# Rooms by rank: sorting the experts of a routed layer on the chip and giving each a room of its own size

## The chip, the core and the metric

The kernel runs on one core of a Trainium2 chip. The metric is the time of one execution in device microseconds (us); the time before is 1312.08 us, the median of three runs (1309.42 to 1315.21).

The engines of the core, by the names that the profile uses: PE is TensorE's matmul, PEld its weight load, DVE is VectorE, ACT is ScalarE, POOL is GpSimd, SP is SyncE, which issues most of the DMAs. Each engine executes its own stream in order; a letter q behind a name (SPq) is the engine's sequencer.

## The reference

Three stages, one after another, all in float32.

1. Attention of 4 batches, 8 heads, 576 positions, head size 64. In each row of scores only the 32 largest are kept before the softmax.
2. A gated layer: with x of 2304 tokens by 512, `(x @ w_a) * (x @ w_b) @ w_out`, inner width 1536.
3. A routed layer with 8 experts. Each token goes to the expert whose embedding is nearest in direction; its output is scaled by the softmax weight of that expert:

```
expert_idx = np.argmax(logits, axis=1)
gate_w = probs[np.arange(N), expert_idx]
for e in range(E):
    mask = expert_idx == e
    h = np.maximum(x[mask] @ w1[e], 0.0)          # w1[e]: 512 x 1024
    out[mask] = gate_w[mask, None] * (h @ w2[e])  # w2[e]: 1024 x 512
```

How many tokens an expert gets is known only when the routing has run.

## The kernel before, in words

Attention and gated layer are interleaved: the attention's scores, top-32 search and softmax set a step order that the program writes out by hand for PE, DVE, ACT and POOL, and matmuls of the gated layer (groups of 256 tokens, `moe1`) fill PE's gaps. All products are made of three float32r products of high and low parts (`TERMS`).

When a chunk of 128 tokens leaves the gated layer, `route` (L760) runs in small steps between other work, 18 chunks in all. It stores the row in `xr`, computes norms, logits, the softmax sum, the expert, and the token's rank in its expert from a running count `base8` (128 equal rows of 8 counts). The row with its softmax sum in column `DM` goes to DRAM (`row_d`, L801), and its token number is scattered by an indirect DMA (L819) into the list of its expert, `ids_d`, which has 2560 places per expert.

Then the experts run, in a second part in which only PE's order is by hand; the order of the other engines and of SP's queue comes from a scheduler that plays the program through in an estimated time and lets instructions move ahead of others where their inputs are there, by priority.

- `first_expert` (L1154) computes the first 256 tokens of expert 0, which are known before the last chunks are routed.
- `last_tile` (L1222) computes the rest of expert 0's room, rows 256 to 335. It also gathers the rows of the next expert (`gather`, L1216, three indirect DMAs by `pick`) and turns them (`turn_x`, L1103: four PE transposes, an ACT copy of the high part, a DVE subtraction for the low part).
- The loop at L1269 does experts 1 to 7 with a room of `cap` = 336 columns each. Stage 1 (`stage1`, L1126) has 8 blocks of 12 matmuls, weights stationary, `cap` columns moving; stage 2 (L1284) has 4 blocks of 24 with `cap` columns and, in the last expert alone, tiles of tokens stationary (`stage2`). Results of the others are turned back (`back`) in the next expert's stage 1.
- `put` (L1114) takes the reciprocal of the softmax sum (DVE, L1115), scales the result on ACT and scatters the rows to the output by an indirect DMA on POOL. Rows past an expert's count are dummies: they read a zero row and are dropped in the scatter.
- Weights come in units of 1 MB, four per expert, through two raw buffers (`unit`, L1047; DMA on SP at L1061, for the first four in quarters at L1058), and ACT and DVE split them into high and low parts in four buffers `u`. `upto` starts units four ahead.
- The ids of all experts are loaded by seven DMAs on SP (L1212) when the last scatter of `ids_d` has landed.
- At the end a loop guarded by a register (L1353, `more`) computes tiles of any expert that has more than 336 tokens (`extra`). With the reference's inputs it does not run.

## Time and profile before

| | us |
|---|---|
| median of the runs | 1312.08 |
| profiled execution | 1318.34 |
| its span | 1316.50 |
| PE busy / PEld busy | 1170.2 / 1008.8 |
| DVE, ACT, POOL busy | 933.3, 819.9, 726.1 |
| DMA moved | 240.58 MB, mean 183 GB/s |

The span is that of the profiler's records, from the first to the last. Three stretches can be told apart: to about 870 us the attention, with DVE busy nearly all of the time; to about 1050 us the rest of the gated layer and the first tiles of expert 0; from 1081 to 1306 us experts 1 to 7. Busy time of PE counts overlapping matmuls by a modelled end, so the pace of matmuls is read from the distance of their starts. The granted clock is in parts of 2.4 GHz: 1.00 is 2.4 GHz, 0.50 is 1.2 GHz.

### The profile page before, as it was taken

How to read it: one execution, taken by the hardware profiler on the slowest of the kernel's cores; microseconds unless marked ns; L12 is line 12 of the kernel's file. 1: busy time of each engine (PE TensorE's matmuls, PEld its weight loads, DVE VectorE, ACT ScalarE, POOL GpSimd, SP SyncE). 2: the span in 40 equal slices, each digit the busy share in tenths (PEclk: the TensorE clock that was granted, in tenths of full speed). 3: DMA queues.
4: the chain of work that ended last, by engine and by line, in shares of the span. 5: the costliest groups of instructions: out<-in, count | busy, mean ns of one | idle time of the engine just before them, and what ended most of it. 6: DMA issues, size and time to landing. Idle time of an engine off the chain costs nothing. (4 is left out here: it accounts for less than half of the span.)

```text
span 1316.5 us, 23808 instructions
## 1 busy us (share of the span) xinstructions
PE 1170.2 (89%) x8124; PEld 1008.8 (77%) x8125; DVE 933.3 (71%) x2019; ACT 819.9 (62%) x1964; POOL 726.1 (55%) x1188
## 2 busy tenths in 40 slices
PE   5667978879999987999998998899999989999996
PEld 3445655667888766888887886777988869999995
DVE  8998998989889889999988898740200136555550
ACT  5876888777767776777777776663532335444441
POOL 5655886667667775676777766564544320222211
PEclk8887999989999997999999999899999989999998
DMA  7433775557686645667665767458987045555530
GB/s 227 141 108 123 249 234 179 193 166 216 201 248 184 178 151 180 194 195 204 199 191 160 213 185 213 128 158 277 333 285 232 32 125 169 176 175 175 177 113 23
DMA packets 129102, 240.58 MB, mean 183 GB/s; under 512 B 24621, under 2 KB 73901, under 8 KB 128978
## 3 DMA queue, kind: packets, MB, share of 16 engines
q1 hardware_dynamic: 124818, 228.74, 56.1%
q0 software_dynamic: 4160, 10.29, 2.2%
q8 instruction: 65, 1.06, 0.3%
q14 instruction: 59, 0.48, 0.1%
HBM read 198.92 MB, written 40.85 MB: 182 GB/s over the span
## 5 line engine op out<-in xcount | busy, mean ns | idle before, releaser
L387 DVE MAX8 t<-y 128x8 f32<-128x576 f32 x432 | 312.2, 750 | 3.0
L402 POOL TENSOR_TENSOR z<-s,z 128x576 f32<-128x576 f32 x144 | 206.2, 1432 | 105.0 <-ACT z L399 100.2
L390 DVE MATCH_REPLACE8 y<-t,y 128x576 f32<-128x576 f32 x288 | 213.9, 743 | 0.0
L722 PE MATMUL ab<-xg,wab 128*128 128x256 f32 x1398 | 205.6, 289 | 7.4 <-ACT gab L736 3.1
L722 PEld LDWEIGHTS ab<-xg,wab 128*128 128x128 f32 x1398 | 181.8, 190 | 11.3 <-ACT gab L736 3.5
L722 PE MATMUL ab<-raw,wab 128*128 128x256 f32 x1152 | 173.4, 291 | 8.1 <-ACT gab L736 5.0
L421 PE MATMUL tr<-ident,z 128*128 128x128 f32 x720 | 133.6, 285 | 37.2 <-ACT z L404 31.2
L722 PEld LDWEIGHTS ab<-raw,wab 128*128 128x128 f32 x1152 | 151.7, 192 | 12.3 <-ACT gab L736 5.9
L404 ACT ACTIVATE z<-z,bi 128x576 f32<-128x576 f32 x144 | 111.7, 775 | 69.9 <-POOL z L402 69.9
L366 PE MATMUL tr<-kT,qT 128*128 128x288 f32 x512 | 128.0, 333 | 25.8 <-ACT qT L343 13.7
L387 DVE MAX8 t<-s 128x8 f32<-128x576 f32 x144 | 107.6, 747 | 51.5 <-ACT s L367 43.2
L367 ACT ACTIVATE s<-tr 128x288 f32<-128x288 f32 x288 | 119.0, 414 | 33.4 <-PE tr L366 32.1
L424 ACT ACTIVATE wt<-tr 128x384 f32<-128x384 f32 (+2 forms) x320 | 128.0, 415 | 16.3 <-PE tr L421 15.6
L1117 POOL DMA_INDIRECT out_dram<-o,ids x24 | 31.4, 1307 | 190.4 <-DVE u L1068 107.1
L669 PE MATMUL x<-wo,gh 128*128 128x512 f32 x432 | 135.8, 395 | 0.0
L656 POOL TENSOR_TENSOR gab<-gab 128x256 f32<-128x256 f32 x108 | 82.6, 765 | 92.1 <-ACT gab L736 80.5
L421 PEld LDWEIGHTS tr<-ident,z 128*128 128x128 f32 x720 | 90.1, 145 | 54.2 <-ACT z L404 35.8
L1068 DVE TENSOR_TENSOR u<-raw,u 128x1024 fp32r<-128x1024 f32 x64 | 75.9, 1222 | 77.6 <-ACT u L1067 55.2
L366 PEld LDWEIGHTS tr<-kT,qT 128*128 128x128 f32 x512 | 87.4, 204 | 38.8 <-ACT qT L343 16.1
L399 ACT ACTIVATE z<-s,bi 128x576 f32<-128x576 f32 x144 | 112.9, 784 | 0.6 <-DVE bi L392 0.6
L1133 PE MATMUL h<-xT,u 128*128 128x336 f32 x672 | 109.3, 319 | 0.0
L656 POOL TENSOR_TENSOR gl<-gab,gh 128x256 fp32r<-128x256 f32 x108 | 80.6, 747 | 49.8 <-ACT gh L656 37.7
(193 smaller groups left out, 2299.8 us busy)
## 6 DMA issues: line engine op xcount, KB each, us to landing
wab<-wab_d SPq DMA_DIRECT2D x192, 512.0 KB, 4.3
raw<-in_moe_w_dram SPq DMA_DIRECT2D x28, 1024.0 KB, 6.5
wab_d<-wab SPq DMA_DIRECT2D x24, 512.0 KB, 4.3
kT<-kT_d SPq DMA_DIRECT2D x20, 576.0 KB, 7.7
vs<-in_v_dram SPq DMA_DIRECT2D x36, 256.0 KB, 3.5
kT_d<-kT SPq DMA_DIRECT2D x16, 576.0 KB, 4.0
raw<-in_moe_w_a_dram SPq DMA_DIRECT2D x12, 512.0 KB, 4.2
raw<-in_moe_w_b_dram SPq DMA_DIRECT2D x12, 512.0 KB, 5.3
```

The lines of the kernel that those rows point to most:

```text
L366: pe.matmul(p, l, r, start=(i == 0), stop=(i == len(terms) - 1))
L367: act.activation(t.s[:, cs], p, AF.Copy, scale=SCALE)
L387: dve.max(v, cur)
L390: dve.match_replace(out=rest, in_to_replace=v, in_values=cur, imm_value=LOWEST)
L399: act.activation(t.w, t.s, AF.Relu, bias=t.bi[:, 1:2], scale=-HUGE)
L402: pool.tensor_tensor(t.w, t.s, t.w, op=OP.subtract)
L404: act.activation(t.w, t.w, AF.Exp, bias=t.bi[:, 0:1], accum_out=t.o.sm[:, t.slot : t.slot + 1])
L421: pe.transpose(pt[:, i * P : (i + 1) * P], t.w[:, k0 : k0 + P], ident)
L424: act.activation(th[:, sl, w], pv[:, :, src], AF.Copy)
L656: pend.pop(0)[1]()
L669: pe.matmul(px[t], g[:, ts], wo[:, w, f], start=(f == 0 and i == 0), stop=(f == NF - 1 and i == 2))
L722: pe.matmul(ps_[i], wt[:, a, c, :], xg[x][:, c, :], start=(j == 0 and f not in begun), stop=(j == len(terms) - 1),)
```

## The change

- Experts 1 to 7 are put in the order of their counts. With the last `base8` DVE forms a key, 8 x count + number, for each expert; expert 0 gets a key above all. One instruction sorts the eight keys in falling order; the lowest three bits are the expert's number.
- SP loads the seven numbers into registers (`values_load`, at the highest priority). The ids of the sorted experts are loaded with a register in the address, one DMA for each expert, and so are their weights (`unit`).
- Each place in the order has a room: `CAPS` = 336 for expert 0, then 336, 328, 312, 296, 280, 272, 264. Place 7, the smallest, runs first, place 1 last.
- The reciprocal of the softmax sum moves from `put` into `route`: the row in DRAM now holds the factor itself. The DVE instruction stands one step later in the routing than the sum, and the row's DMA behind it.
- The overflow test at the end compares each place's count with its room, and the guarded loop runs over places.

```diff
@@ -23,6 +23,8 @@
 LOWEST = -3.0e38
 STRIDE = 2560
 CAP = 336
+CAPS = (CAP, 336, 328, 312, 296, 280, 272, 264)
+FIRST = 2.0**20
 GROUPS = [(256 * i, 256) for i in range(9)]
 GN = 256
 SEQ = "0A 0B 1A 0T 1BT 2A 2BT 3AT 3B"
...
@@ -142,6 +144,9 @@
     pool.iota(e8i, pattern=[[1, NE]], base=0, channel_multiplier=0)
     e8 = cst.tile([P, NE], F32, name="e8")
     dve.tensor_copy(e8, e8i)
+    e8k = e8i.bitcast(F32)
+    dve.tensor_copy(e8k, e8)
+    dve.memset(e8k[:, 0:1], FIRST)
     e8s = cst.tile([P, NE], F32, name="e8s")
     dve.tensor_scalar(e8s, e8, float(STRIDE), None, op0=OP.mult)
 
...
@@ -797,14 +802,15 @@
             pool.tensor_copy(ohb, oh)
             yield 0.0
             pool.memset(xr[:, DM + 1 : RW], 0.0)
-            pool.tensor_tensor(xr[:, DM : DM + 1], st[:, 3:4], eps, op=OP.add)
-            sp.dma_start(row_d[1 + ch * P : 1 + (ch + 1) * P, :], xr)
+            pool.tensor_tensor(st[:, 6:7], st[:, 3:4], eps, op=OP.add)
             pr = mp.tile([P, 512], F32, name="ab", bufs=2)
             pe.matmul(pr[:, 0:NE], tri, ohb, start=True, stop=True)
             pe.matmul(pr[:, NE : 2 * NE], ones, ohb, start=True, stop=True)
             rk = mk.tile([P, 2 * NE], F32, name="rk")
             act.activation(rk, pr[:, 0 : 2 * NE], AF.Copy)
             yield 0.0
+            dve.reciprocal(xr[:, DM : DM + 1], st[:, 6:7])
+            sp.dma_start(row_d[1 + ch * P : 1 + (ch + 1) * P, :], xr)
             pool.tensor_tensor(rk[:, :NE], rk[:, :NE], base8, op=OP.add)
             pool.tensor_tensor(base8, rk[:, NE:], base8, op=OP.add)
             if ch == NCL - 1:
...
@@ -1046,12 +1052,13 @@
 
         def unit(i, pace=False):
 
-            e, part = divmod(i, 4)
+            n, part = divmod(i, 4)
+            e = slice(0, 1) if n == 0 else bass.ds(expert[NE - n], 1)
             raw = w2p.tile([P, 4, 512], F32, name="raw", bufs=2)
             if part < 2:
-                src = w1[e, :, part * 512 : (part + 1) * 512].rearrange("(c p) f -> p c f", p=P)
+                src = w1[e, :, part * 512 : (part + 1) * 512].rearrange("o (c p) f -> p (o c) f", p=P)
             else:
-                src = w2[e, (part - 2) * 512 : (part - 1) * 512, :].rearrange("(f p) d -> p f d", p=P)
+                src = w2[e, (part - 2) * 512 : (part - 1) * 512, :].rearrange("o (f p) d -> p (o f) d", p=P)
             if pace:
                 for c in range(4):
                     act.activation(raw[:, c, 0:1], recent[0][:, 0, 0:1], AF.Copy)
...
@@ -1081,8 +1089,12 @@
         wx = ph.enter_context(tc.tile_pool(name="wx", bufs=1, side="right"))
         banks = [ph.enter_context(tc.tile_pool(name="ps2", bufs=1, space=PSUM, side="right"))]
         TERMS = ((1, 0), (0, 1), (0, 0))
+        cap = max(caps)
         NT3 = -(-cap // P)
-        M = [min(P, cap - t * P) for t in range(NT3)]
+
+        def rows_of(r):
+
+            return [min(P, caps[r] - t * P) for t in range(NT3)]
         idv = ids_d.rearrange("(e r) c -> e r c", e=NE)
         turns = {"h": 0, "y": 0, "tr": 0}
 
...
@@ -1112,8 +1124,7 @@
             dve.tensor_tensor(lo, pv, hi.bitcast(F32), op=OP.subtract)
 
         def put(p, xg, ids, m, o):
-            dve.reciprocal(xg[:m, DM + 1 : DM + 2], xg[:m, DM : DM + 1])
-            act.activation(o[:m], p[:m], AF.Copy, scale=xg[:m, DM + 1 : DM + 2])
+            act.activation(o[:m], p[:m], AF.Copy, scale=xg[:m, DM : DM + 1])
             pool.indirect_dma_start(
...
@@ -1207,28 +1218,41 @@
             return
 
         wk = ph.enter_context(tc.tile_pool(name="wk2", bufs=2))
-        for es, ts in ((slice(0, 1), (NT3 - 1,)), (slice(1, 2), range(NT3)), (slice(2, NE), range(NT3))):
-            for t in ts:
-                sp.dma_start(ids[: M[t], es, t, :], idv[es, t * P : t * P + M[t], :].rearrange("e p c -> p e c"))
+        m0 = rows_of(0)[-1]
+        sp.dma_start(ids[0][:m0, NT3 - 1], idv[0, (NT3 - 1) * P : (NT3 - 1) * P + m0, :])
+        key = wx.tile([P, 2, 8], F32, name="key")
+        counts = wx.tile([P, 8], I32, name="counts")
+        place = wx.tile([P, 8], I32, name="place")
+        with tc.high_priority(offset=FG):
+            dve.scalar_tensor_tensor(key[:, 0], base8, 8.0, e8k, op0=OP.mult, op1=OP.add)
+            dve.max(key[:, 1], key[:, 0])
+            dve.tensor_copy(counts, key[:, 1])
+            dve.tensor_scalar(place, counts, 7, None, op0=OP.bitwise_and)
+            for r in range(NE - 1, 0, -1):
+                expert[r] = nc.values_load(place[0:1, r : r + 1], engines=[sp.engine], min_val=0, max_val=NE - 1)
+        for r in range(NE - 1, 0, -1):
+            sp.dma_start(
+                ids[r], idv[bass.ds(expert[r], 1), : NT3 * P, :].rearrange("o (t p) c -> p (o t) c", p=P)
+            )
 
         banks.append(ph.enter_context(tc.tile_pool(name="ps3", bufs=1, space=PSUM)))
 
-        def gather(e):
+        def gather(r):
             xs = [wx.tile([P, RW], F32, name="xg", bufs=2 * NT3) for _ in range(NT3)]
             for t in range(NT3):
-                pick(xs[t], t, ids[: M[t], e, t, 0:1])
-            return xs, [wk.tile([P, KC, cap], F32R, name=f"xT{i}") for i in range(2)]
+                pick(xs[t], ids[r][: rows_of(r)[t], t, 0:1])
+            return xs, [wk.tile([P, KC, cap], F32R, name=f"xT{i}")[:, :, : caps[r]] for i in range(2)]
 
         def last_tile():
 
-            t, m = NT3 - 1, M[-1]
+            t, m = NT3 - 1, m0
             xs = [None] * t + [wx.tile([P, RW], F32, name="xg", bufs=2 * NT3)]
-            xT = [wk.tile([P, KC, cap], F32R, name=f"xT{i}") for i in range(2)]
+            xT = [wk.tile([P, KC, cap], F32R, name=f"xT{i}")[:, :, : caps[0]] for i in range(2)]
             hT = [wk.tile([P, NF2, cap], F32R, name=f"hT{i}", bufs=1)[:, :, :m] for i in range(2)]
-            pick(xs[t], t, ids[:m, 0, t, 0:1])
-            nx = gather(1)
+            pick(xs[t], ids[0][:m, t, 0:1])
+            nx = gather(NE - 1)
             turn_x((xs, xT), t)
...
@@ -1254,35 +1278,37 @@
             for f in range(NF2):
                 stage2(0, f, p, hT[0][:, f], hT[1][:, f])
                 if f in FX:
-                    turn_x(nx, 1 + FX.index(f))
-            put(p, xs[t], ids[:m, 0, t, 1:2], m, result())
+                    turn_x(nx, 1 + FX.index(f), NE - 1)
+            put(p, xs[t], ids[0][:m, t, 1:2], m, result())
             return nx
 
-        def back(e, xs, yT, t):
-            m = M[t]
+        def back(r, xs, yT, t):
+            m = rows_of(r)[t]
...
+            hT = [wk.tile([P, NF2, cap], F32R, name=f"hT{i}", bufs=1)[:, :, :n] for i in range(2)]
             for f in range(NF2):
                 if f % 4 == 0:
                     upto(4 * e + f // 4 + UB)
-                for _ in stage1(e, f, xT, hT[0][:, f], hT[1][:, f], cap):
+                for _ in stage1(e, f, xT, hT[0][:, f], hT[1][:, f], n):
                     pass
                 if backs and f % 2 == 0:
                     backs.pop(0)()
                 if f == GF and e + 1 < NE:
-                    nx = gather(e + 1)
+                    nx = gather(r - 1)
             if e + 1 < NE:
-                yT = wx.tile([P, KC, cap], F32, name="yT", bufs=1)
+                yT = wx.tile([P, KC, cap], F32, name="yT", bufs=1)[:, :, :n]
                 for d in range(KC):
-                    p = bank("y")[:, :cap]
+                    p = bank("y")[:, :n]
                     for f in range(NF2):
                         if f % 4 == 0 and d == 0:
                             upto(4 * e + 2 + f // 4 + UB)
...
@@ -1338,24 +1364,27 @@
                 pe.matmul(p, hT[:, f, :], w2f[:, f, :], start=(f == 0), stop=(f == NF2 - 1))
             put(p, xg, ids[:, 1:2], P, result())
 
-        top = wk.tile([P, 8], F32, name="top", bufs=1)
-        dve.max(top, base8)
-        NX = -(-(NT - cap) // P)
-        need = wk.tile([P, NE, NX], I32, name="need", bufs=1)
-        lim = wk.tile([P, NX], I32, name="lim", bufs=1)
-        pool.iota(lim, pattern=[[P, NX]], base=cap, channel_multiplier=0)
-        limf = wk.tile([P, NX], F32, name="limf", bufs=1)
-        dve.tensor_copy(limf, lim)
-        for e in range(NE):
-            dve.tensor_scalar(need[:, e, :], limf, base8[:, e : e + 1], None, op0=OP.is_lt)
-        more = wk.tile([P, 1], I32, name="more", bufs=1)
-        dve.tensor_scalar(more, top[:, 0:1], float(cap), None, op0=OP.is_gt)
-        with tc.If(nc.values_load(more[0:1, 0:1], min_val=0, max_val=1) > 0):
-            with tc.For_i(0, NE, 1) as e:
-                with tc.For_i(0, NX, 1) as t:
-                    go = nc.values_load(need[0:1, bass.ds(e, 1), bass.ds(t, 1)], min_val=0, max_val=1)
-                    with tc.If(go > 0):
-                        extra(e, t)
+        starts = wx.tile([P, 8], I32, name="starts")
+        over = wx.tile([P, 8], I32, name="over")
+        for r, c in enumerate(caps):
+            pool.iota(starts[:, r : r + 1], pattern=[[0, 1]], base=c, channel_multiplier=0)
+        dve.tensor_scalar(over, counts, 3, None, op0=OP.logical_shift_right)
+        dve.tensor_scalar(over[:, 0:1], over[:, 0:1], int(FIRST) // 8, None, op0=OP.subtract)
+        dve.tensor_tensor(over, over, starts, op=OP.subtract)
+        dve.tensor_scalar(over, over, 0, None, op0=OP.max)
+        dve.tensor_copy(key[:, 0], over)
+        dve.max(key[:, 1], key[:, 0])
+        dve.tensor_copy(counts, key[:, 1])
+        with tc.If(nc.values_load(counts[0:1, 0:1], min_val=0, max_val=NT) > 0):
+            with tc.For_i(0, NE, 1) as r:
+                with tc.For_i(0, -(-(NT - min(caps)) // P), 1) as t:
+                    left = nc.values_load(over[0:1, bass.ds(r, 1)], min_val=0, max_val=NT)
+                    with tc.If(left > t * P):
+                        e = nc.values_load(place[0:1, bass.ds(r, 1)], engines=[sp.engine], min_val=0, max_val=NE - 1)
+                        first = nc.values_load(
+                            starts[0:1, bass.ds(r, 1)], engines=[sp.engine], min_val=min(caps), max_val=max(caps)
+                        )
+                        extra(e, first, t)
 
 
 _INS = ["q", "k", "v", "moe_w_a", "moe_w_b", "moe_w_out", "moe2_expert_emb", "moe2_tau", "moe2_w1", "moe2_w2"]
```

## Rows read from the trace of the kernel before

**Rows 1.** Busy by windows: us, PE PEld DVE ACT POOL (instructions), clock, DMA.
```profile
1100.00:1150.00 50.00, 50.00 (x338) 49.84 (x337) 27.05 (x40) 21.47 (x32) 9.17 (x8) 1.00 0.46 154
1250.00:1300.00 50.00, 50.00 (x311) 47.80 (x310) 19.34 (x31) 17.35 (x28) 8.17 (x7) 1.00 0.25 88
```
**Rows 2.** Timeline of PE: start, us, engine, line, operation, out<-in, sizes, count.
```profile
1041.63 6.65 PE L1133 MATMUL h<-xg,u 128*128 128x256 f32 x54
1048.11 5.75 PE L1145 MATMUL y<-u,wab 128*128 128x512 f32 x24
1053.69 5.74 PE L1145 MATMUL h<-u,wab 128*128 128x512 f32 x24
...
1081.21 14.88 PE L1133 MATMUL h<-xT,u 128*128 128x336 f32 x96
1095.94 4.80 PE L1291 MATMUL y<-hT,u 128*128 128x336 f32 x30
```
**Rows 3.** Timeline of PE, transposes of a third tile.
```profile
1108.87 0.44 PE L1108 MATMUL tr<-ident,xg 80*128 80x80 f32 x4
1109.11 3.03 PE L1291 MATMUL y<-hT,u 128*128 128x336 f32 x18
```
**Rows 4.** Timeline of PE at the seam; in brackets the idle time before.
```profile
1060.73 1.14 PE L1239 MATMUL h<-u,xT 128*80 128x512 f32 x4
1066.66 6.67 PE L1239 MATMUL h<-u,xT 128*80 128x512 f32 x20 [4.79 <-DVE xT L1112]
1073.16 0.44 PE L1246 MATMUL tr<-ident,o 80*128 80x80 f32 x4
```
**Rows 5.** Timeline of DVE there: first and last of six reciprocals, then the subtraction.
```profile
1058.51 0.16 DVE L1115 RECIPROCAL xg<-xg 80x1 f32<-80x1 f32 x1 [9.35 <-DMA xg<-row_d,ids]
...
1065.38 0.16 DVE L1115 RECIPROCAL xg<-xg 128x1 f32<-128x1 f32 x1 [1.35 <-DMA xg<-row_d,ids]
...
1066.12 1.08 DVE L1112 TENSOR_TENSOR xT<-tr,xT 128x320 fp32r<-128x320 f32 x2
```
**Rows 6.** Windows at the seam, columns as in rows 1.
```profile
1064.00:1067.00 3.00, 0.34 (x1) 0.34 (x2) 1.31 (x6) 0.00 (x0) 0.17 (x1) 0.50 0.37 151
1067.00:1070.00 3.00, 3.00 (x8) 1.75 (x7) 1.57 (x10) 0.00 (x0) 1.02 (x2) 0.50 0.19 74
1070.00:1075.00 5.00, 4.25 (x22) 2.67 (x21) 1.72 (x2) 2.90 (x5) 0.00 (x0) 0.93 0.00 0
```
**Rows 7.** Timeline of POOL: the last counts, the first gather.
```profile
1044.04 0.20 POOL L809 TENSOR_TENSOR base<-rk,base 128x8 f32<-128x8 f32 x1
...
1055.29 0.94 POOL L1095 DMA_INDIRECT xg<-row_d,ids  x1 [6.58 <-issue]
```
**Rows 8.** Line L1353 on SP: durations in ns, first and last start.
```profile
L1353 SPq TENSOR_LOAD <-more x1: 479/479/479, 1066.3 to 1066.3; - x1
L1353 SPq FUSED_REGOPS  x1: 177/177/177, 1066.9 to 1066.9; - x1
...
L1353 SPq COMPARE_BRANCH  x1: 45/45/45, 1262.7 to 1262.7; - x1
```
**Rows 9.** Timeline of SP: weights of units 4 and 5, last rows, ids.
```profile
943.95 0.38 SPq L1061 DMA_DIRECT2D raw<-in_moe_w_dram  x1
...
960.62 0.38 SPq L1061 DMA_DIRECT2D raw<-in_moe_w_dram  x1
...
1038.51 2.34 SPq L801 DMA_DIRECT2D row_d<-xr  x2
1052.51 3.40 SPq L1212 DMA_DIRECT2D ids<-ids_d  x7
```
**Rows 10.** Line L1061, the weight loads of 1 MB, from issue.
```profile
DMA to landing us min/median/max: 5.0/6.5/10.4
```
**Rows 11.** Timeline of DVE in the attention phase: a routing step.
```profile
415.66 0.15 DVE L784 RECIPROCAL st<-st 128x1 f32<-128x1 f32 x1
415.73 0.15 DVE L786 MAX8 m<-lg 128x8 f32<-128x8 f32 x1
```

More of the change, by code (lines that the diff above doesn't have):

```diff
@@ L99, in fused_kernel @@
     batches=4,
-    cap=CAP,
+    caps=CAPS,
 ):
@@ L1071, in fused_kernel @@
         units = {}
+        expert = [0] * NE
         def upto(i):
@@ L1091, in bank, with pick @@
             return banks[turns[name] % len(banks)].tile([P, 512], F32, name=name, bufs=2 if name == "h" else 1)
-        def pick(xg, t, idx, src=row_d):
+        def pick(xg, idx, src=row_d):
             pool.indirect_dma_start(
-                out=xg[: M[t]],
+                out=xg[: idx.shape[0]],
                 out_offset=None,
@@ L1101, in pick, with turn_x @@
             return xg
-        def turn_x(x, t):
+        def turn_x(x, t, r=0):
             xs, xT = x
-            m = M[t]
+            m = rows_of(r)[t]
             pt = bank("tr")
@@ L1150, in result @@
             return wx.tile([P, DM], F32, name="o", bufs=OB)
-        ids = wx.tile([P, NE, NT3, 2], I32, name="ids")
+        ids = [wx.tile([P, NT3, 2], I32, name=f"ids_{r}") for r in range(NE)]
         def first_expert():
@@ L1159, in first_expert @@
             for t in range(2):
-                pick(xs[t], t, ids[:, t, 0:1], row_d[: 1 + NCL * P])
+                pick(xs[t], ids[:, t, 0:1], row_d[: 1 + NCL * P])
             yield 0.0
@@ L1229, in last_tile @@
-            nx = gather(1)
+            pick(xs[t], ids[0][:m, t, 0:1])
+            nx = gather(NE - 1)
             turn_x((xs, xT), t)
-            turn_x(nx, 0)
+            turn_x(nx, 0, NE - 1)
             hs = []
@@ L1256, in last_tile @@
                 if f in FX:
-                    turn_x(nx, 1 + FX.index(f))
-            put(p, xs[t], ids[:m, 0, t, 1:2], m, result())
-            return nx
-        def back(e, xs, yT, t):
-            m = M[t]
+                    turn_x(nx, 1 + FX.index(f), NE - 1)
+            put(p, xs[t], ids[0][:m, t, 1:2], m, result())
+            return nx
+        def back(r, xs, yT, t):
+            m = rows_of(r)[t]
             pt = bank("tr")
@@ L1265, in back @@
                 pe.transpose(pt[:m, d * P : (d + 1) * P], yT[:, d, t * P : t * P + m], ident)
-            put(pt, xs[t], ids[:m, e, t, 1:2], m, result())
+            put(pt, xs[t], ids[r][:m, t, 1:2], m, result())
         x, backs = last_tile(), []
         for e in range(1, NE):
+            r = NE - e
+            n, M = caps[r], rows_of(r)
             nx = None
             xs, xT = x
-            hT = [wk.tile([P, NF2, cap], F32R, name=f"hT{i}", bufs=1) for i in range(2)]
+            hT = [wk.tile([P, NF2, cap], F32R, name=f"hT{i}", bufs=1)[:, :, :n] for i in range(2)]
             for f in range(NF2):
@@ L1298, in fused_kernel @@
                         if f == XF and d:
-                            turn_x(nx, d - 1)
+                            turn_x(nx, d - 1, r - 1)
                     dve.tensor_copy(yT[:, d], p)
-                backs = [partial(back, e, xs, yT, t) for t in range(NT3)]
+                backs = [partial(back, r, xs, yT, t) for t in range(NT3)]
             else:
@@ L1309, in fused_kernel, with extra @@
                         stage2(e, f, p, hT[0][:, f, ts], hT[1][:, f, ts])
-                    put(p, xs[t], ids[: M[t], e, t, 1:2], M[t], result())
+                    put(p, xs[t], ids[r][: M[t], t, 1:2], M[t], result())
             x = nx
         order.__exit__(None, None, None)
-        def extra(e, t):
+        def extra(e, first, t):
             ids = wk.tile([P, 2], I32, name="ids2", bufs=1)
-            sp.dma_start(ids, ids_d[bass.ds(e * STRIDE + t * P + cap, P), :])
+            sp.dma_start(ids, idv[bass.ds(e, 1), bass.ds(first + t * P, P), :].rearrange("o p c -> p (o c)"))
             xg = wx.tile([P, RW], F32, name="xg", bufs=2 * NT3)
```

## The prediction

> **What bounds the kernel now.** I read the busy shares over the last 270 us first, then TensorE's timeline there, then VectorE's, and last what SyncE's queue and POOL issue at the seam between the first expert and the others.
>
> From 1100 to 1300 us TensorE has no idle time: 50.00 of 50 us in each stretch, at granted clock 1.00 (2.4 GHz), while VectorE is busy 27 to 19 of 50 us, ScalarE 21 to 17 and the DMA engines 0.46 to 0.25 [rows 1]. So in the seven experts whose rooms change, the end is set by the number of matmuls times their spacing, and nothing else is late.
>
> At the seam this is not so. TensorE issues four matmuls of the last tile of expert 0 at 1060.73 us and then sits 4.79 us until VectorE writes the low part of xT [rows 4]. VectorE had only small work in that time: six reciprocals of `put`, from 1058.51 to 1065.38, each of which waits for a gather to land, because they were put into VectorE's order ahead of that subtraction at 1066.12 [rows 5]. After the stall the granted clock is 0.50 (1.2 GHz) from 1064 to 1070 us and 0.93 to 1075 [rows 6]: the engine had been idle, and the next 20 matmuls pay for it too.
>
> **Part 1, the columns.** Rooms fall from 336 to 336, 328, 312, 296, 280, 272, 264 for the seven sorted experts: 8+24+40+56+64+72 = 264 columns less. Each column passes 96 matmuls in stage 1 (8 blocks of 12) and 96 in stage 2 (4x8x3); the expert that keeps 336 is the last one, whose stage 2 has another form. The spacing at 336 columns is (1095.94-1081.21)/96 = 153.4 ns, at 256 columns (1048.11-1041.63)/54 = 120.0 ns [rows 2]: 33.4/80 = 0.418 ns per column, and the two ends enclose every new size. Saving: 264 x 192 x 0.418 = 21.2 us. All of it is on the path, since TensorE is what is late [rows 1]. The four transposes of a third tile of 80 rows hold TensorE 0.24 us [rows 3]; with 72 to 8 rows they cost between nothing and that, six times: 0 to 1.4 us less, I take half, 0.7.
>
> What could be late next: the smallest expert takes 192 x 123.3 ns = 23.7 us, and some 2 us of transposes, six sets of four. Its weights are four loads of 1 MB, 6.5 us to landing at the median [rows 10]; even one after another they need 26 us, and there are two raw buffers. VectorE at 27 of 50 us has, in the 32 us that an expert takes now (192 x 153.4 ns and the transposes), some 17 us of work, part of which shrinks. I see no new bound.
>
> The Trainium skill (TensorE: Matmul & The Clock Gate, Back-to-back issue gap) speaks against this part: with a weight load per matmul it gives a sustained 81 ns at 128 columns and 131 ns at 512, 0.13 ns per column, by which the saving would be an estimated 6.6 us. The trace does not agree: 24 matmuls of 512 columns with a weight load each took 5.58 us from 1048.11 to 1053.69, 232 ns apiece [rows 2].
>
> **Part 2, the reciprocals.** Out of `put` go 24 of VectorE (0.16 us each [rows 5]); in the steady stretch they were worth nothing, at the seam they were the stall. Without them the subtraction can follow ScalarE's copy at once, as VectorE has nothing else there. TensorE then goes on at about 1061.7, and the 20 matmuls run at 232 ns = 4.65 us instead of the 6.50 us from 1066.66 to 1073.16 [rows 4]. Gain: 4.8 + 1.85 = 6.6 us, if nothing else comes late.
>
> In exchange 18 reciprocals of one column stand in the routing. VectorE in the attention phase has no gaps; the routing's existing reciprocal at 415.66 delays the next instruction by 0.07 us and lasts 0.15 [rows 11]. About 12 of the 18 fall into that full phase: 12 x 0.1 = 1.2 us, bounds 0 and 12 x 0.15 = 1.8, if POOL's addition of 1e-9, issued one routing step earlier, is done by then. The row write to DRAM moves behind it by a step on SyncE's queue; weight blocks queued behind it could wait, which I price at 0 to 2 us and take as 0, because the step's wait is short against the double-buffered blocks.
>
> **Part 3, the sort.** It needs the last `base8`, written at 1044.04 + 0.20 us [rows 7]. Four small VectorE operations follow; at 0.15 to 0.2 us each [rows 11], with the first expert's evictions between them, the places exist at 1045 to 1047. Then SyncE loads seven registers. The one load that the trace shows took 0.479 + 0.177 = 0.66 us [rows 8]; seven are 4.6 us, so 1050 to 1052. Hidden by: SyncE's wait for the last token ids to land, which ends only at 1052.51 [rows 9]. The cover is about 1 us wide. Then come the ids: eight loads instead of seven, seven of them with a register in the address. No row shows such a load; the nearest is the register operation of 0.177 us beside seven plain issues in 3.40 us [rows 8, 9]. Added per load: 0 to 0.7 us. The gather of the next expert's first tile needs the second of the eight, so it slips by 0 to 2 us; I take 0.8, and TensorE waits for that tile just after POOL's first gather (1055.29 [rows 7]). Seam in all: 6.6 - 0.8 = 5.8 us gained, bounds -2 and 7.
>
> The first two weight loads of the sorted experts were issued at 943.95 and 960.62, far ahead [rows 9]. They can't be any more: they need the register. They now run from 1052 at the earliest or about 1058, behind the ids. Needed: the first at about 1066, when its buffer and ScalarE come free, the second 3 us later. With 6.5 us to landing [rows 10] they come by 1059 to 1067. I cost this at 0, at most 3 us. What their absence gives to the transfers around 944 and 961 us is not counted.
>
> The 28 weight loads by register cost SyncE perhaps 0.18 us each [rows 8], in an expert of 26 us or more with four of them: nothing. The overflow test at the end (eight iotas, seven small VectorE operations, one register load per engine as before) finds POOL idle 6.58 us before its first gather [rows 7] and VectorE idle 9.35 us before 1058.51 [rows 5]; nothing, or 1 us if an iota ends up behind a scatter.
>
> **Sum.** 21.2 + 0.7 + 5.8 - 1.2 = 26.5 us. The profiled execution took 1318.34 us (span 1316.50, 1.84 around it): 1291.8. It lies 6.3 us above the median of the runs, 1312.08; taking the same difference from the median gives 1285.6, so 1286.
>
> **The rivals.**
> Late registers. If the seven register loads stand behind the ids load of expert 0 on SyncE, which waits until 1052.51, the next expert's ids are asked for only at 1052.9 + 4.6 = 1057.5, 4.6 us later than now, and the gather and TensorE's wait for it move by the same. The stall that the reciprocals made is then made by the gather, with its half clock: gain 21.9 - 1.2 = 20.7 us, 1291; with the weights late as well, up to 4 us more, 1295. For it: SyncE executes in order and issued nothing between its row writes at 1038.51 to 1040.85 and the ids at 1052.51 [rows 9], where the wait for expert 0's ids could stand first. Against: the sort is given the highest priority in the queue, and its data are there first.
>
> A pace that does not follow the columns, because the weight load of each matmul sets it. For it: TensorE's weight loads are busy 49.84 of 50 us [rows 1]. Against: 120.0 ns at 256 columns [rows 2]. By a third of the slope 7 us are saved, in all about 12: 1300. That is also where the skill's spacing would put it.
>
> Something other than TensorE ends last in the small experts (weight conversion, gathers): half of the columns' gain or none remains, 1296 to 1307. Against: the busy shares [rows 1].
>
> Overflow, the slower side. The reference's own inputs give 271 tokens to expert 0 and, sorted, 327, 326, 303, 287, 268, 262, 260 to the others; all fit, by 2 to 12 rows. The point from which it decides is one token above a room (the tightest: 326 in 328). Then the loop over 8 x 16 places runs, each with a register load and a branch of 0.66 + 0.05 us [rows 8] at least: 128 x 0.71 = 91 us, and the extra tile's own work: 1312 - 27 + 91 = 1376 or more. Before, 336 held every expert with 9 to spare. Against: tokens would have to change expert through rounding.
>
> **How the numbers follow.** Forecast 0.63 (1280 to 1292 by itself), late registers 0.20, pace 0.05, other bound 0.07, overflow 0.05. From 1278 to 1299 lie nearly all of the first two and a part of the next two: 0.85. A change of 0.5% (6.6 us) is about what a measurement of this kernel can tell. Faster: the first three and most of the fourth, 0.91; within: 0.04, where the other bound takes all but the seam; slower: overflow, 0.05.
>
> **What would show it.** Right: the spacing of the matmuls falls expert by expert from 123 ns to 153; TensorE stays without gaps from the second sorted expert on; no reciprocal and no idle of 4.8 us after the fourth matmul of the last tile, clock 1.00 there; SyncE's seven register loads end before 1052. Wrong: the ids of the sorted experts asked for after 1056; TensorE waiting for a gather or for the first weights at the seam; waits for weights inside the small experts; any instruction of the overflow loop.

## The result and the profile after

The changed kernel took 1292.13 us (median, 1291.03 to 1296.71); the kernel before, run beside it, 1313.97 us. Ratio 0.9828, 95% interval 0.98 to 0.9855; run again unchanged it gave 0.9794 [0.975, 0.9839]. Predicted were 1286 us and 26.5 us of gain.

The two profiled executions are 27.4 us apart in span (1316.5 and 1289.1). I cut each at TensorE's starts: the *start* up to the last 54 matmuls of expert 0's stage 1, the *seam* up to stage 1 of the next expert, the *experts* up to the last 72 matmuls, the *tail*.

| us | start | seam | experts | tail |
|---|---|---|---|---|
| before | 1041.63 | 39.58 | 207.84 | 27.45 |
| after | 1039.27 | 36.41 | 186.28 | 27.14 |
| gain | (2.36) | 3.17 | 21.56 | 0.31 |
| predicted | -1.2 | 5.8 | 21.9 | 0 |

The start says little: the first reciprocal of the routing, ahead of which the kernels differ by two small VectorE instructions at most, stands at 283.26 to 289.71 us in the profiles, 6.5 us apart. The other three stretches repeat closely from run to run; together they gained 25.0 us, 1.9%, which both ratios hold. The median of the first comparison says 21.8.

TensorE after, from the seam to the smallest expert (timeline, columns as in [rows 2]):
```profile
1057.11 0.44 PE L1120 MATMUL tr<-ident,xg 80*128 80x80 f32 x4
1059.86 0.66 PE L1120 MATMUL tr<-ident,xg 128*128 128x128 f32 x4 [2.32 <-DMA xg<-row_d,ids]
1060.28 7.34 PE L1263 MATMUL h<-u,xT 128*80 128x512 f32 x24
1067.45 0.44 PE L1270 MATMUL tr<-ident,o 80*128 80x80 f32 x4
...
1075.68 11.84 PE L1144 MATMUL h<-xT,u 128*128 128x264 f32 x96
1087.36 2.33 PE L1317 MATMUL y<-hT,u 128*128 128x264 f32 x18
...
1090.41 1.74 PE L1317 MATMUL y<-hT,u 128*128 128x264 f32 x12 [0.72 <-DVE hT L1149]
...
1098.80 0.41 PE L1120 MATMUL tr<-ident,xg 16*128 16x16 f32 x4
1099.15 2.44 PE L1317 MATMUL y<-hT,u 128*128 128x264 f32 x18
```
This is to be seen against [rows 2, 3, 4]. The 24 matmuls are one group now, the 4.79 us inside it are gone; but ahead of it stand 2.32 us of waiting for the gather of the next expert's first tile, and the group lasts 7.17 us instead of the 5.58 of a group of 24 in [rows 2]. The 96 matmuls at 264 columns take 11.68 us, 121.7 ns each (153.4 before). The 0.72 us is the one new stall in the small experts. The four transposes of a third tile hold TensorE longer with 16 rows than with 80, 0.35 us instead of 0.24.

Windows after (columns as in [rows 1]):
```profile
1054.00:1057.00 3.00, 3.00 (x15) 2.43 (x14) 0.00 (x0) 0.00 (x0) 2.39 (x3) 1.00 0.83 207
1057.00:1060.00 3.00, 0.68 (x7) 0.44 (x6) 0.49 (x1) 1.12 (x2) 2.09 (x3) 1.00 1.02 380
1060.00:1064.00 4.00, 4.00 (x14) 2.53 (x14) 0.69 (x1) 0.60 (x1) 1.04 (x1) 0.59 1.06 395
1064.00:1067.00 3.00, 3.00 (x15) 1.94 (x14) 0.54 (x1) 1.54 (x2) 0.00 (x0) 0.98 0.25 93
...
1080.00:1090.00 10.00, 9.69 (x80) 9.48 (x79) 7.85 (x12) 6.17 (x11) 0.00 (x0) 1.00 0.66 223
1100.00:1150.00 50.00, 50.00 (x403) 49.62 (x402) 30.06 (x43) 27.27 (x43) 13.52 (x12) 1.00 0.63 211
1200.00:1250.00 50.00, 50.00 (x352) 49.88 (x351) 27.47 (x37) 23.00 (x34) 9.87 (x8) 1.00 0.45 151
```
In the kernel before, while the same gather was under way:
```profile
1057.00:1060.00 3.00, 2.78 (x16) 2.13 (x15) 0.25 (x2) 0.53 (x1) 2.38 (x3) 1.00 0.72 168
```
From 1057 to 1064 us the DMA engines are full now (1.02, 1.06 at 380 to 395 GB/s), where they had been busy 0.72 at 168 GB/s. While TensorE waits there the granted clock is still 1.00; in the stretch behind it 0.59, so that part of the 24 matmuls ran at 1.2 GHz. In the small experts TensorE is as full as in [rows 1], the others busier.

SyncE's queue, timeline and then the register line L1232 and the ids line L1234 with durations in ns:
```profile
1049.51 0.35 SPq L1222 DMA_DIRECT2D ids<-ids_d  x1
1050.07 3.76 SPq L1234 DMA_DIRECT2D ids<-ids_d  x7
1054.02 0.99 SPq L1068 DMA_DIRECT2D raw<-in_moe_w_dram  x2
```
```profile
L1232 SPq TENSOR_LOAD <-place x7: 261/273/472, 1043.2 to 1047.2; - x7
L1232 SPq FUSED_REGOPS  x7: 147/147/181, 1043.7 to 1047.6; - x7
...
L1234 SPq DMA_DIRECT2D ids<-ids_d x7: 372/373/420, 1050.1 to 1053.5; - x7
```
POOL's first two gathers (timeline):
```profile
1052.46 0.94 POOL L1107 DMA_INDIRECT xg<-row_d,ids  x1 [6.50 <-DMA ids<-ids_d]
1053.71 0.99 POOL L1107 DMA_INDIRECT xg<-row_d,ids  x1 [0.30 <-issue]
```
The seven registers are there at 1047.7 us, before the ids of expert 0 could be asked for at 1049.51; the sorted ids' issues took 3.76 us for seven against 3.40 in [rows 9], 0.05 us more each; the two rows of loads differ in shape too, so this is not the price of the register address alone. Then, 0.3 us after the gather that TensorE will wait for, two weight loads of 1 MB go out at 1054.02. That gather, issued by 1054.70, let TensorE go on at 1059.86, 5.2 us later; in the profile of before the same step took 2.4 us (issued by 1057.52, transposes at 1059.93).

VectorE at the seam and in the attention phase (timeline):
```profile
1042.95 0.16 DVE L1371 TENSOR_SCALAR over<-counts 128x8 int32<-128x8 int32 x1
...
1044.35 0.17 DVE L1377 CAST counts<-key 128x8 int32<-128x8 f32 x1
...
1058.55 0.49 DVE L1124 TENSOR_TENSOR xT<-tr,xT 128x320 fp32r<-128x320 f32 x1 [11.54 <-ACT xT L1123]
```
```profile
419.26 0.16 DVE L812 RECIPROCAL xr<-st 128x1 f32<-128x1 f32 x1 [1.92 <-POOL st L805]
```
No reciprocal stands ahead of the subtraction [rows 5]. The overflow test, whose register was loaded at 1066.3 us before [rows 8], is over on VectorE at 1044.5. In the attention phase the new reciprocal waits for POOL, here 1.92 us, 9.8 us in all over five of the steps there.

### The profile page after: what moved, and what is told of

Same layout as the page of the kernel before. It is cut to its first block, busy times and chain, and to the rows that moved or that the text cites. A ratio compares the mean times of both kernels' runs of the same rounds, so it can differ in the third digit from the quotient of the medians.

```text
span 1289.1 us, 23877 instructions
## 1 busy us (share of the span) xinstructions
PE 1152.1 (89%) x8124; PEld 989.9 (77%) x8125; DVE 920.5 (71%) x2015; ACT 817.3 (63%) x1964; POOL 727.0 (56%) x1195
## 3 DMA queue, kind: packets, MB, share of 16 engines
q8 instruction: 65, 1.06, 0.3%
## 5 line engine op out<-in xcount | busy, mean ns | idle before, releaser
L395 DVE MATCH_REPLACE8 y<-t,s 128x576 f32<-128x576 f32 x144 | 106.9, 743 | 0.0
```

What stands on the lines that cost most here:

```text
L395: dve.match_replace(out=rest, in_to_replace=v, in_values=cur, imm_value=LOWEST)
```

## The experiments

The theory after the result: the columns came as predicted; at the seam the two weight loads, issued now right behind the gathers, slow the gather's landing. The rival: the reciprocals were not worth what I priced, and the seam's gain is from elsewhere. The kernel before, run beside each of three groups of them, took 1318.73, 1319.02 and 1318.66 us, so ratios are compared; stretches come from each profile.

| kernel | median us | ratio [95%] | seam | experts |
|---|---|---|---|---|
| e1_factors | 1318.51 | 0.999 [0.9968, 1.0012] | 38.71 | 207.84 |
| e2_rooms336 | 1314.95 | 0.9972 [0.9954, 0.9989] | 36.43 | 207.84 |
| e3_hold | 1292.66 | 0.981 [0.9781, 0.984] | 36.30 | 185.85 |
| e4_early | 1289.84 | 0.9791 [0.9755, 0.9826] | 33.75 | 186.40 |
| after_again | 1290.96 | 0.9794 [0.975, 0.9839] | 36.22 | 186.49 |
| e7_limits | 1316.83 | 0.9999 [0.9975, 1.0023] | 38.39 | 207.54 |
| e6_put | 1302.08, one run | | 36.19 | 194.39 |
| e8_hold4 | 1292.03 | 0.9816 [0.9769, 0.9863] | 33.66 | 188.18 |
| e12_turn4 | 1291.88 | 0.9802 [0.9776, 0.9827] | 33.87 | 186.49 |
| e10_turn | 1295.28, one run | | 37.59 | 185.63 |
| e11_limits | 1315.35, one run | | 32.91 | 207.84 |
| e5_over | 1776.91, one run | | | |

**e2_rooms336**: the change without its rooms.
```diff
-CAPS = (CAP, 336, 328, 312, 296, 280, 272, 264)
+CAPS = (CAP,) * 8
```


> The changed kernel with all eight rooms at 336: sort, registers and factors in rows stay, the columns come back. If the columns are the whole gain of the experts' stretch, it goes from 186.28 back to 207.8 us, the seam stays at about 36.4, and the time is 21.6 us above the changed kernel, 2 to 3 us under the kernel before (ratio 0.998). Rival: loads by register or the order by size have a share of their own; then the experts' stretch differs from 207.8 by more than 1 us.


The experts take 207.84 us again, to the hundredth those of before; the seam stays at 36.43. So the 21.56 us are the rooms, columns and transposes together, and sort, registers and addresses cost nothing in the experts.

**e1_factors**: the kernel before with the factors in rows alone.
```diff
-            pool.tensor_tensor(xr[:, DM : DM + 1], st[:, 3:4], eps, op=OP.add)
-            sp.dma_start(row_d[1 + ch * P : 1 + (ch + 1) * P, :], xr)
+            pool.tensor_tensor(st[:, 6:7], st[:, 3:4], eps, op=OP.add)
...
+            dve.reciprocal(xr[:, DM : DM + 1], st[:, 6:7])
+            sp.dma_start(row_d[1 + ch * P : 1 + (ch + 1) * P, :], xr)
...
-            dve.reciprocal(xg[:m, DM + 1 : DM + 2], xg[:m, DM : DM + 1])
-            act.activation(o[:m], p[:m], AF.Copy, scale=xg[:m, DM + 1 : DM + 2])
+            act.activation(o[:m], p[:m], AF.Copy, scale=xg[:m, DM : DM + 1])
```


> The kernel before with one part of the change alone: the reciprocal of the softmax sum moves into the routing. Stretches are counted by TensorE's starts: seam, from the last 54 matmuls of the first expert's stage 1 to the next expert's stage 1 (39.58 us before, 36.41 in the changed kernel); experts, from there to the last 72 matmuls (207.84 and 186.28). The prediction's step: the six reciprocals were the stall of 4.79 us and the cause of the half clock, so the seam falls to about 33.0 us, the experts stay at 207.8, the routing costs about 1 us; in all 5 to 6 us less than before, ratio 0.996. Rival: the stall was the gathers' own lateness and only showed up behind the reciprocals; then the seam stays at 38 to 40 us and the ratio is 1.00.


No gain. The old stall is gone, but 10 us later stands a new one. POOL, VectorE and TensorE of e1_factors:
```profile
1071.80 1.00 POOL L1117 DMA_INDIRECT out_dram<-o,ids  x1 [3.04 <-ACT u L1068]
1072.80 0.18 POOL L1346 IOTA lim<- 128x16 int32 x1
```
```profile
1073.02 0.17 DVE L1348 CAST limf<-lim 128x16 f32<-128x16 int32 x1 [6.22 <-POOL lim L1346]
```
```profile
1065.28 5.76 PE L1239 MATMUL h<-u,xT 128*80 128x512 f32 x24
...
1076.01 1.57 PE L1145 MATMUL y<-u,hT 128*80 128x512 f32 x3 [3.28 <-DVE hT L1250]
```
The 24 matmuls run through, as I had predicted for the change. But the overflow test's iota stands behind a result's scatter in POOL's order, VectorE waits for it 6.22 us with work of expert 0 queued behind, and TensorE 3.28.

**e7_limits** and **e11_limits** move that test in e1. In e7 it stands at the head of the phase with high priority:
```diff
         wk = ph.enter_context(tc.tile_pool(name="wk2", bufs=2))
+        with tc.high_priority(offset=FG):
+            top = wk.tile([P, 8], F32, name="top", bufs=1)
...
+            pool.iota(lim, pattern=[[P, NX]], base=cap, channel_multiplier=0)
```


> The kernel before with the factors in rows, and in addition the overflow test (its iota on GpSimd and its VectorE operations) moved ahead of the gathers. With the factors alone the seam was 38.71 us: the old stall was gone, but VectorE then waited 6.22 us for an iota that stood behind a result scatter on GpSimd, and TensorE 3.28 us for VectorE. Theory: the reciprocals and the overflow test held VectorE one behind the other; without both the seam is 32.5 to 33.5 us, as the prediction had it for the reciprocals alone, ratio 0.995. Rival: a third wait of about the same length takes over; seam above 36 us.


In e11 the iota and its copy have high priority, and their tiles lie in `wx`, the memory that holds `ids` too:
```diff
+        lim = wx.tile([P, NX], I32, name="lim", bufs=1)
+        limf = wx.tile([P, NX], F32, name="limf", bufs=1)
+        with tc.high_priority(offset=FG):
+            pool.iota(lim, pattern=[[P, NX]], base=cap, channel_multiplier=0)
+            dve.tensor_copy(limf, lim)
```


> The kernel before with the factors in rows, and the overflow test's iota and its conversion now in memory that is free early (the pool of the expert stage) and at high priority. In the run before, moving them in the program alone did not help: the iota's tile lay in memory that the gated layer gives back only after the first expert, so GpSimd put it behind six gathers and a scatter, VectorE waited 3.48 us for it and TensorE 3.88 for VectorE. Theory: without it the seam is 32.5 to 33.5 us, the 6.6 us that the prediction gave the reciprocals alone. Rival: another wait of VectorE takes its place, seam above 36.


VectorE of e7, then TensorE of e11:
```profile
1059.24 0.18 DVE L1218 CAST limf<-lim 128x16 f32<-128x16 int32 x1 [3.48 <-POOL lim L1216]
```
```profile
1064.41 5.92 PE L1245 MATMUL h<-u,xT 128*80 128x512 f32 x24 [0.58 <-ACT xT L1112]
```
Moving it in the program did little: the iota still ran at 1059.00, behind six gathers and a scatter, and TensorE waited 3.88 us; seam 38.39. In other memory, both waits are gone: 32.91, 6.67 us less than before. That is the 6.6 us that I had priced for the reciprocals, to 0.1; it takes both edits. Both had high priority; e11's iota also stands ahead of the first expert in the program, so e11 alone does not tell place from memory. The changed kernel does: its eight iotas stand behind all the experts, without priority, but in `wx`, and they ran as early as e11's. The iotas of e11, then of the changed kernel (first and last start):
```profile
L1157 POOL IOTA lim<- x1: 163/163/163, 901.8 to 901.8; 128x16 int32 x1
L1370 POOL IOTA starts<- x8: 147/147/156, 896.4 to 896.9; 128x1 int32 x8
```

**e6_put**: the change with the reciprocals back in `put` (the three edits of e1 undone).


> The changed kernel with the reciprocals back in the result step (24 on VectorE after each gather), the rows holding the sum again. If the reciprocals hold VectorE at the seam also here, where the gathers land later because of the weight loads, the subtraction that TensorE waits for comes after the sixth gather's landing: idle 6 to 9 us after the fourth matmul of the last tile, half clock behind it, seam 42 to 45 us against 36.4. Rival: with the overflow test out of the way the scheduler puts the subtraction first; seam within 1 us of 36.4, and the move of the factor is worth nothing at the seam.


The seam is 36.19 again, but by another wait. VectorE, then TensorE, of e6_put at the seam:
```profile
1064.59 0.16 DVE L1126 RECIPROCAL xg<-xg 128x1 f32<-128x1 f32 x1 [3.72 <-DMA xg<-row_d,ids]
1064.99 1.09 DVE L1123 TENSOR_TENSOR xT<-tr,xT 128x320 fp32r<-128x320 f32 x2 [0.24 <-issue]
```
```profile
1065.54 4.84 PE L1263 MATMUL h<-u,xT 128*80 128x512 f32 x20 [2.64 <-DVE xT L1123]
1070.22 0.44 PE L1270 MATMUL tr<-ident,o 80*128 80x80 f32 x4
```
Three of the six reciprocals stand ahead of the subtraction, and TensorE waits 2.64 us for it behind the fourth matmul, as in the kernel before. No wait for the first gather shows: the weight loads went out 0.7 us behind it (1056.96 and 1056.23), 0.3 in the changed kernel. The 20 matmuls took 4.68 us, at a granted clock of 1.00 all through. So the equal seam is two waits in exchange, not reciprocals that cost nothing. The experts took 194.39 us, 8.1 more. VectorE, then TensorE, in a small expert of e6_put:
```profile
1151.92 0.15 DVE L1126 RECIPROCAL xg<-xg 40x1 f32<-40x1 f32 x1 [5.11 <-DMA xg<-row_d,ids]
1152.00 0.42 DVE L1149 SCALAR_TENSOR_TENSOR hT<-h,hT 128x280 fp32r<-128x280 f32 x1
```
```profile
1152.47 2.47 PE L1317 MATMUL y<-hT,u 128*128 128x280 f32 x9 [3.15 <-DVE hT L1149]
```
A reciprocal waits 5.11 us for its gather, the low half of hT queued behind it, and TensorE 3.15 us for that; 6.5 us in four such places (0.76 of them where the changed kernel waits 0.72), and a granted clock of 0.99 over the experts. With 336 columns there was room for this, with 280 there is none.

**e3_hold** and **e8_hold4** keep the two weight loads back until the first tile is gathered.
```diff
+                if hold[0] is not None:
+                    act.activation(raw[:, 0, 0:1], hold[0], AF.Copy)
                 sp.dma_start(raw, src)
...
+            hold[0] = nx[0][0][:, 0:1]
             upto(2 + UB)
+            hold[0] = None
```


> The changed kernel with the first two weight loads of the sorted experts held back until the first gathered tile of that expert has landed (a one-column copy on ScalarE from that tile into the raw buffer before the load). Theory (shared DMA): at the seam the gathers are issued early enough, but two loads of 1 MB are issued 0.3 us after the first of them and take the DMA engines, so the tile lands 5.2 us after its issue ended instead of 2.4, TensorE idles 2.32 us and the clock falls. Then here the idle is under 0.5 us, the 24 matmuls after it take 5.6 us instead of 7.2, and the seam is 32.5 to 33.5 us instead of 36.4. Rival (late ids): the gather is late because its ids come later than before through registers; then holding the weights changes nothing, idle about 2 us and seam 36, or it is longer because the weights come late too.


TensorE of e3_hold, then ScalarE:
```profile
1058.12 5.75 PE L1266 MATMUL h<-u,xT 128*80 128x512 f32 x24 [0.58 <-issue]
1066.51 0.79 PE L1273 MATMUL tr<-ident,o 80*128 80x80 f32 x4 [2.36 <-ACT o L1269]
```
```profile
1065.86 0.59 ACT L1269 ACTIVATE o<-h 80x512 f32<-80x512 f32 x1 [2.34 <-DMA out_dram<-o,ids]
```
The theory holds for its place: without the loads the wait is 0.58 us and the 24 matmuls run at full clock. But the loads now meet the scatter of a result (issued at 1059.47), whose buffer ScalarE needs: 2.34 us, half clock again (0.57 from 1066 to 1070), seam 36.30. e8_hold4 takes that buffer away too:
```diff
+            yT = wx.tile([P, KC, cap], F32, name="yT", bufs=1).rearrange("p c j -> p (c j)")
...
-                hs.append(result())
+                hs.append(yT[:, half * 512 : half * 512 + 512])
```


> The kernel with held weights (first two weight loads wait for the first gathered tile), and in addition the two hidden halves of the last tile are kept in the tile for turned results, which is free then, instead of in two of the three result buffers. With held weights alone the idle before the last tile fell from 2.32 to 0.58 us and its 24 matmuls ran at full clock, but a result scatter then shared the DMA engines with the weights, its buffer came free late, ScalarE waited 2.34 us for it and TensorE 2.36. Theory: that wait is the rest; without it the seam is 32.5 to 33.5 us. Rival: the weights themselves come too late when held back; seam above 35 us with TensorE waiting for the weight split.


Seam 33.66, 2.75 us better; but the weights come late now. ScalarE, then TensorE, of e8_hold4:
```profile
1070.74 2.96 ACT L1077 ACTIVATE u<-raw 128x1024 fp32r<-128x1024 f32 x3 [1.88 <-DMA raw<-in_moe_w_dram]
```
```profile
1092.09 1.75 PE L1323 MATMUL y<-hT,u 128*128 128x264 f32 x12 [1.56 <-DVE hT L1152]
```
In that last place the changed kernel waits 0.72 us. The experts give back 1.9 us.

**e4_early** asks for the two loads as soon as the first register is there:
```diff
                 expert[r] = nc.values_load(place[0:1, r : r + 1], engines=[sp.engine], min_val=0, max_val=NE - 1)
+                if r == NE - 1:
+                    begin(4)
+                    begin(5)
```


> The changed kernel with the same two weight loads moved ahead: they are issued right after the first of the seven register loads, in the 5 us in which SyncE otherwise waits for the last scatter of token ids to land. Theory (shared DMA): they are through before the gathers, idle under 0.5 us, seam 32.5 to 33.5 us, if the scatter's landing is not slowed in turn; if it is (same DMA engines), the ids are asked for 1 to 3 us later than 10.2 us after the start of the last 54 matmuls, and the idle of 1 to 3 us comes back by that way. Rival (late ids): no change, idle 2.3 us, seam 36.4.


SyncE of e4_early, then TensorE:
```profile
1046.29 1.66 SPq L1067 DMA_DIRECT2D raw<-in_moe_w_dram  x2
...
1053.28 0.36 SPq L1235 DMA_DIRECT2D ids<-ids_d  x1
```
```profile
1060.86 0.66 PE L1133 MATMUL tr<-ident,xg 128*128 128x128 f32 x4 [0.81 <-DMA xg<-row_d,ids]
1061.27 5.75 PE L1279 MATMUL h<-u,xT 128*80 128x512 f32 x24
```
Seam 33.75, and nothing given back: 2.5 us under the change in seam and experts together, the best sum beside e12's 2.3. Not free either: the loads slowed the scatter that the ids wait for. The ids were asked for 5.35 us after its issue ended (1047.93 in e4) instead of 3.55 (1045.96 in the change), so 11.91 us after the first of the last 54 matmuls instead of 10.24.

**e10_turn** and **e12_turn4** move the transposes of the next tile behind the 24 matmuls, e12 with e8's buffers.
```diff
             turn_x((xs, xT), t)
-            turn_x(nx, 0, NE - 1)
...
+            turn_x(nx, 0, NE - 1)
```


> The same move of the four transposes alone, with the hidden halves left in the result buffers. If the result scatter, which shares the DMA engines with the weight loads, frees its buffer late here as it did with held weights (ScalarE waited 2.34 us), TensorE waits 1.5 to 2.5 us between the two halves' transposes and the seam is 34.5 to 36 us; if not, it is as with both edits, 32.5 to 33.5.

> The changed kernel with the four transposes of the next expert's first tile moved on TensorE behind the 24 matmuls of the last tile of expert 0, which need only the first gather; and the two hidden halves of the last tile in the tile for turned results instead of two result buffers. Theory (shared DMA): the weights may keep the gather late, as long as nothing waits for it; 5.6 us of matmuls now stand in front, so the idle of 2.1 to 2.3 us and the half clock behind it go, seam 32.5 to 33.5 us instead of 36.3, experts 186.3 as before, so 3 us less than the changed kernel and ratio 0.977 to the kernel before. Rival: the next thing is late by as much (the first tile's low part on VectorE, the weight split), seam above 35.


TensorE of e10_turn:
```profile
1072.10 0.49 PE L1270 MATMUL tr<-ident,o 80*128 80x80 f32 x4 [3.29 <-DVE xT L1124]
```
In e10 TensorE does not wait for the gather, but behind the 24 matmuls: the scatter that ScalarE's result buffer waits for (3.33 us) is late too, beside the weights' transfers as in e3; seam 37.59. In e12 waits of 1.01 and 1.18 us remain, 33.87.

**after_again** is the change, for the spread beside these.


> The changed kernel once more, beside the others on this chip. By stretches: seam 36.4 us, experts 186.3, tail 27.1 as in its first profile, since these have no other load on them; the time from the first routing step to the end of the top-32 search within 2 us of 586. The stretch before the first routing step, in which nothing that matters was changed, moves by up to 5 us from one execution to the next, so the difference of the medians to the kernel before is 22 to 25 us although the two first profiles differed by 27.4. Rival: those 27.4 us are the change; then the ratio is 0.979.


Its seam of 36.22 and experts of 186.49 differ by 0.2 from the first profile; so the 2.5 us of e4, e8 and e12 at the seam are beyond that. In the medians none is told from the change: 1289.84, 1292.03, 1291.88 beside 1290.96, with intervals of 0.5%.

**e5_over** prices the slower side with one room too small for six tokens:
```diff
-CAPS = (CAP, 336, 328, 312, 296, 280, 272, 264)
+CAPS = (CAP, 336, 320, 312, 296, 280, 272, 264)
```


> The changed kernel with the third room at 320 instead of 328 columns, so that the expert with 326 tokens has six too many and the guarded loop runs. The prediction's price: 128 passes of at least 0.71 us and one extra tile, 91 us or more above the changed kernel: 1380 us or more. Rival: the passes cost far more because each loads a register on five engines and they meet at every branch: 128 x 2 to 3 us, 1550 to 1700 us.


The loop's 128 passes and the one extra tile cost 485 us over the change (1776.91 - 1292). The tile itself, from its ids' load at 1402.30 to its result's scatter at 1431.94, is some 30 us of them, which leaves about 3.5 us per pass. Windows of the loop:
```profile
1300.00:1750.00 450.00, 18.07 (x84) 13.52 (x84) 0.00 (x0) 3.50 (x10) 1.99 (x2) 0.52 0.03 10
```
All engines stand still nearly all of the time.

## Why the prediction was right, and where it was off

- **The columns, right, with small errors that cancel.** 21.9 predicted, 21.56 measured, and e2 gives them back to the hundredth. The matmuls alone gave 22.8 us (195.8 to 173.0 in the experts' stretch, by the distances of their starts): 121.7 ns at 264 columns, where I had 123.3. The third tiles' transposes, for which I took 0.7 us off, cost 0.5 us more (six sets, 1.91 us instead of 1.44), and the stall of 0.72 us was not in the sum. The rivals of a pace that does not follow the columns and of another bound are refuted; of the second there is a beginning, the 0.72 us in the smallest expert, where VectorE is busy 7.85 of 10 us. The sustained spacings of the Trainium skill (TensorE: Matmul & The Clock Gate, Back-to-back issue gap), by which the saving would have been a third, do not describe these matmuls: 121.7 ns at 264 columns and 153.4 at 336 stand in the trace.
- **The registers, right.** 1045 to 1047 us for the places: 1043.04, which is 1045.4 with the 2.36 us by which this execution's start was shorter. Registers done by 1050 to 1052: 1047.7, so 1050.1; the seven loads took 4.6 us, as priced. A load with a register in its address took 0.05 us more where I gave 0 to 0.7. The rival of late registers did not come about, though the time fell where it had put it.
- **The seam, the term that failed: 5.8 predicted, 3.17 measured.** Two prices were wrong. "I cost this at 0, at most 3 us" for the first two weight loads asked only whether they come in time, which they do. It did not ask what 2 MB do to a transfer already under way: the gather landed 2.8 us later, TensorE waited 2.32 us and the next 24 matmuls ran partly at half clock, 1.59 us. These 3.9 us, less the 0.8 that I allowed, are what is missing to within 0.5 us. TensorE waiting for a gather at the seam was one of my own signs of being wrong, and the clock of 1.00 that I named as a sign of being right was 0.59. e3 shows the cause by removing it, e4 by moving it. The reciprocals' 6.6 us cannot be read from the sum: with them back in `put` the seam is 36.19 too (e6), and they show as 6.67 only in e11, where neither the test nor the loads are in the way. The Trainium skill has the rule (DMA: Bandwidth & Descriptors, Issuing engines are not separate DMA queues): transfers issued by SyncE and by GpSimd run on the same 16 engines and interleave. The runs agree, with 2.4 us against 5.2.
- **The overflow test, "nothing, or 1 us".** Its rewriting was needed: with the old test the same edit gained nothing (e1), with it out of the way 6.67 us (e11). In the changed kernel the iotas' tiles lie in `wx`, where they ran at 896.4 us, and the test runs at 1043 to 1044.5, so the time came out right by a part that I had priced as idle.
- **The reciprocals in the steady stretch, "worth nothing".** True with 336 columns, 8.1 us with the small rooms (e6): the two halves of the change support each other.
- **The routing, 1.2 us, not seen.** From the first routing reciprocal to the end of the attention's selection on VectorE the kernel before needs 586.0 us; with the new routing it is 586.7 (after), 586.9 (after_again), 587.3 (e1) and 584.1 (e2), over all the runs with it 583.4 to 590.7: the spread hides it. The reciprocal does wait for POOL, which I had made a condition.
- **Overflow, refuted as an event, mis-sized as a price.** 91 us at least, from one register load and one branch per pass; measured 485, since a pass costs about 3.5 us and not 0.71.
- **From gain to time.** 26.5 predicted, 25.0 in the stretches that repeat, 21.8 and 28.1 in two comparisons of medians. I carried the gain over to a median of 1312.08 of three runs; the start alone moves by 6.5 us between executions. 1286 and 1292.13 differ by 2.6 us of the seam; the other 3.5 I put down to this spread. So the time is in part luck: 1292.13 lies just outside the 1280 to 1292 of the forecast by itself and beside the 1291 of the late registers, which did not come about; the range of 1278 to 1299 held because it covered both.

## What to carry to other kernels

Where a change makes a load later, look at what is in flight where it goes now, not only at when it must arrive: a small gather on the critical path pays for megabytes issued 0.3 us behind it. An operation that holds nobody up at one tile size can do so at a smaller one, and an unchanged sum can hide one wait in place of another, so edits that look independent are tried alone and together. And an instruction without inputs is not early because it stands early in the program: its place in the engine's order decides, and here that followed from the memory of its output.

## What the runs showed of the hardware

- TensorE went on with a gather of 128 rows 2.4 us after its issue among other gathers only (168 GB/s) and 5.2 us beside two loads of 1 MB (380 to 395 GB/s).
- A register load takes SyncE 0.261 to 0.479 us, and seven in a row stand 0.67 us apart. Seven DMAs with a register in their address took 0.36 us more to issue than seven without, of another shape.
- A pass of a loop in which five engines each load a register and branch costs about 3.5 us, in which no engine does other work.
- An idle time of 2.3 us on TensorE was followed by a granted clock of 0.59 for 4 us, though it had been 1.00 while idle; waits of 0.58 and 0.81 us were followed by groups of 24 at full pace (5.75 us). The length of the wait alone does not settle it: behind 2.61 us in e2 a group of 24 took 6.72 us, behind 2.64 us in e6 the 20 matmuls took 4.68 at 1.00.
